# The first batch without split operands and in a new written order, and the last tile's ending in halves

## The chip, the cores and the metric

The kernel runs on one core of one Trainium2 chip. The metric is device microseconds of one execution, the median over runs. A core has TensorE (PE, matmuls from SBUF into PSUM), VectorE (DVE), ScalarE (ACT), GpSimd (POOL) and SyncE (SP, which issues most DMAs here). Each engine works through its own queue in order, and waits on semaphores for what others produce.

## The reference

```python
def _attn_ref(q, k, v, p):                  # 8 batches, 8 heads, 576 tokens, 64 wide; p: 32 packing queries
    def sm_attn(qq, kk, vv):
        s = scale * np.matmul(qq, kk.transpose(0, 1, 3, 2))
        s = s - np.max(s, axis=-1, keepdims=True)
        a = np.exp(s)
        a = a / (np.sum(a, axis=-1, keepdims=True) + 1e-09)
        return np.matmul(a, vv)
    p_packed = sm_attn(p, k, v)             # 32 x 64 per head
    return sm_attn(q, p_packed, p_packed)

def _moe_ref(x, w_ch1, w_ch2):              # x: 8 x 576 x 512, the heads side by side
    X = np.fft.fft(np.fft.fft(x, axis=1), axis=2)
    u = x + np.real(X).astype(np.float32)
    mu = np.mean(u, axis=-1, keepdims=True)
    var = np.mean((u - mu) ** 2, axis=-1, keepdims=True)
    un = (u - mu) / np.sqrt(var + 1e-06)
    ch = np.maximum(un @ w_ch1, 0.0) @ w_ch2     # 512 -> 2048 -> 512
    return u + ch
```

## The kernel before

**Tiles.** Every two batches give nine blocks of 128 rows of `u`; four blocks make a tile of 512 rows, so the eight batches make nine tiles. For each tile `ffn` runs 16 steps: `up` (L910, 12 matmuls into the PSUM bank `ph`), Relu into a high part `hh` (ACT) and a low part `hl` (DVE, L917), and `down` of the step before (L927, 12 matmuls into `acc0` to `acc3`). All of this is fp32r (one pass) with each operand split into a rounded high part and the rest: three matmuls stand for one. The helper `split` (L107 copies the high part on ACT, L110 subtracts on DVE or POOL) makes the parts; `wsplits` makes those of the weights (`wr_h`, `wr_l`). After the last step the block is scaled and added (L975, DVE) and stored (L976, SP's queue).

**The front.** `front(b)` makes the blocks of batch b: scores of the packing queries (`s`), their exponentials (`e`), turned by PE (`e1tp`, `e1tq`, copied into `e1T`), packed values (`po`, `pp`), transposed (`pptp`, copied into `ppT`), scores of the 576 queries (`s2T`, turned by DVE into `s`), maximum `m`, exponentials, sum `z`, mean `d`, weights turned back (`a`). Everything comes for two groups g of four heads. Even and odd folds (`eo`, `f`) of the weights take the place of the first transform; `pg` times `turn` gives the spectrum of the packed values (`turned`, joined pairwise into `gh`, `gl`). Products `py` of folds and value spectra, summed over both groups (`first_products`, L702 to L708), give `yh`, `yl` and a remainder `yr`; these times the tables `tbh`, `tbl`, `tbr` give the spectra `pz` (L280 to L282, L632), copied to SBUF (`spec`). The plain values `px` (folds times the spread packed values `bdh`, `bdl`) and the spectra make `pe`, `qe`, and from these the four row blocks in `ubuf` with their row sums (L774 to L783). ACT subtracts the mean (`un`, L994), PE turns the block (`untp`), ACT and DVE split it (`uh`, `ul`), and the first `up` starts.

**What sets the order.** For batches 1 to 7 the front is spread over the steps of the tile ahead. For batch 0 nothing runs yet, and the strings of `ORDER` write the order of PE, DVE, ACT and POOL out by hand: a letter is a part (`parts`), the number its group or argument. Letters used below: `s x t p b d` scores, exponentials, turned scores, packed values, their spread, their transpose; `q e m a` second scores, less maximum, less mean, weights; `g j` value spectrum and its join; `f r` folds and the folds' rest; `h H F J n l` low and high parts; `P X` first products and first values; `w v` two ways to unpack a weight chunk (ACT, DVE), `W K V Q` loads; `i` idle matmuls (`i203`: 20 of them, gated by entry 3 of `gates`), which compute nothing that is used. `T0` to `T2` load tables by POOL's DMA queue. The order of SP's queue is not written by hand. The work on weight chunks is spread over batch 0's front and the first tile (`TOPS`, `BITS`, `fetch`).

PSUM has eight banks: `bank` hands out `acc0` to `acc3` and three others in turn during the first batch; `ph` is single.

Of the kernel before, what the change touches and what calls it, by code (L numbers as in the profile page):

```python
# [83 lines left out]
def tile_kernel(ctx, tc, kpT, qT, v, w1, w2, tabH, tabL, tabR, tabF, tabB, tabT, sel, ident_d, out):  # L84
# [199 lines left out]
    def front(b):  # L284
# [130 lines left out]
        def packed(g):  # L415
# [30 lines left out]

            in_place("b", g, spread)

        def packed_parts(g):
# [7 lines left out]
            hi = work.tile([P, P], F32R, tag="pph", name="pph")  # L457
            lo = work.tile([P, P], F32R, tag="ppl", name="ppl")
            nc.scalar.copy(hi, tp[:, :P])
            in_place("l", g, lambda: nc.vector.tensor_tensor(lo, tp[:, :P], hi.bitcast(F32), ALU.subtract))  # L460
            pph[g], ppl[g] = hi, lo
# [32 lines left out]
        def less_mean(g):  # L494

            z = small.tile([P, 18], F32, tag="z18", name="z18")
            d = small.tile([P, 18], F32, tag="d18", name="d18")
            nc.vector.tensor_reduce(z, s2s[g], AX.X, ALU.add)
            nc.vector.tensor_scalar(d, z, 1.0 / NPK, None, ALU.mult)
            nc.vector.tensor_scalar(z, z, float(NPK), 1e-9, ALU.add, ALU.add)  # L500
# [4 lines left out]
        def values_spectrum(g):

            hi = work.tile([P, 2, N2], F32R, tag="gh", name="gh")
            lo = work.tile([P, 2, N2], F32R, tag="gl", name="gl")
# [16 lines left out]
            def join():  # L525
                for t in range(2):
                    TW[TA[min(b, 2)]].tensor_tensor(prod[0][:, t, :], prod[0][:, t, :], prod[1][:, t, :], ops[t])
                if b == 0:
                    nc.scalar.copy(hi, prod[0])
                    late["J", g] = lambda: nc.vector.tensor_tensor(lo, prod[0], hi.bitcast(F32), ALU.subtract)  # L530
                else:
# [15 lines left out]
        def folded(g):  # L547
# [10 lines left out]
            eos[g], fs[g] = eo, f  # L558

        def folded_rest(g):  # L560
# [29 lines left out]
            nc.scalar.activation(xh[g], ec[:, 0:256], AF.Copy, bias=1.0 / 16)  # L590
            oh[g] = work.tile([P, 256], F32R, tag="oh", name="oh")
            nc.scalar.copy(oh[g], oc[:, 0:256])

        def folded_high(g):
            fh[g] = work.tile([P, FW], F32R, tag="fh", name="fh")
            nc.scalar.copy(fh[g], fs[g])

        def folded_parts(g):
# [9 lines left out]

            def low():
                fl[g] = work.tile([P, FW], F32R, tag="fl", name="fl")  # L610
                nc.vector.tensor_tensor(fl[g], f, fh[g].bitcast(F32), ALU.subtract)
# [15 lines left out]
        def spectrum(t, q, tag=None):  # L627
# [3 lines left out]
            three(pz[:, :N2], tbh[t][:, w], tbl[t][:, w], yh[t][:, q, :], yl[t][:, q, :], True, False)  # L631
# [534 lines left out]
```

## Time and profile before

| | |
|---|---|
| median of 3 runs | 965.59 us (965.23 to 966.66) |
| the profiled execution | 964.36 us |
| its span | 962.2 us |
| PE busy | 944.4 us, 98% of the span |
| DVE, ACT, POOL busy | 589.5, 452.3, 463.2 us |
| mean granted PE clock | 0.998 |

The span is the time from the first to the last record; the execution's own time lies some 2 us above it. Rows of a timeline give the start, the length (of a merged row: from the first start to the last end), engine, line, operation, what it writes and reads, and in brackets the idle time of the engine ahead of it and who ended it. A matmul's length includes its way through the array; matmuls in a row start closer together than they are long. A plain f32 matmul appears as two rows (passes).

### The profile page before, as it was taken

What the parts mean: (1) busy time and instruction counts of PE and PEld (TensorE: products, weight loads), DVE (VectorE), ACT (ScalarE), POOL (GpSimd) and SP (SyncE); (2) the same over time, 40 slices, a digit from 0 to 9 for tenths busy, and PEclk for the clock granted to TensorE, in tenths of its full rate; (3) what the DMA queues carried; (4) which work ended last, traced back from release to release, by engine and by line L of the source; (5) the groups of instructions that cost most, each with busy time, mean ns of one, the idle gap of its engine ahead of it and who ended that gap; (6) DMA issues with size and microseconds to landing.
All of it is one profiled execution on the core that took longest, in us unless ns stands there. A gap on an engine that the chain in (4) does not pass through costs nothing.

```text
span 962.2 us, 15191 instructions
## 1 busy us (share of the span) xinstructions
PE 944.4 (98%) x5614; PEld 774.4 (80%) x5614; DVE 589.5 (61%) x1186; ACT 452.3 (47%) x930; POOL 463.2 (48%) x397
## 2 busy tenths in 40 slices
PE   7899999999999999999999999999999999999997
PEld 4777887788778887788778877888778888887886
DVE  5989967684667756794668466874679353123112
ACT  5689564444434444444444444454444443233331
POOL 3156534653555435643465355543555355445442
PEclk9999999999999999999999999999999999999999
DMA  9675125400340016200540045100600011001001
GB/s 358 220 268 190 42 84 164 136 1 1 128 152 37 1 44 209 85 1 25 165 148 0 1 140 166 55 1 23 212 30 23 16 50 44 22 23 45 1 0 44
DMA packets 48777, 80.74 MB, mean 84 GB/s; under 512 B 7088, under 2 KB 28464, under 8 KB 48704
## 3 DMA queue, kind: packets, MB, share of 16 engines
q1 hardware_dynamic: 42480, 69.62, 21.3%
q10 hardware_dynamic: 5184, 8.85, 2.9%
q0 software_dynamic: 1040, 1.31, 0.5%
q8 instruction: 44, 0.72, 0.3%
q14 instruction: 29, 0.24, 0.1%
HBM read 59.45 MB, written 20.32 MB: 83 GB/s over the span
## 4 chain that ended last, share of the span: by engine, by line
PE 93%; DVE 3%; ACT 2%; DMA 1%; issue 1%; ACTq 0%; DVEq 0%
PE acc L927 40%; PE ph L910 40%; PE po L424 1%; PE px L282 1%; PE px L280 1%; PE px L281 1%; PE s2T L329 1%; PE py L282 1%; PE py L280 1%; PE py L281 1%; PE s L329 1%; ACT e L356 1%; PE idle L730 1%; PE pz L653 0%; DMA kp<-kpT 0%
## 5 line engine op out<-in xcount | busy, mean ns | idle before, releaser
L110 POOL TENSOR_TENSOR wr_l<-w2f,wr_h 128x512 fp32r<-128x512 f32 x144 | 188.2, 1307 | 275.8 <-ACT wr_h L107 269.8
L110 POOL TENSOR_TENSOR wr_l<-w1f,wr_h 128x512 fp32r<-128x512 f32 x144 | 200.3, 1392 | 195.2 <-ACT wr_h L107 175.6
L917 DVE SCALAR_TENSOR_TENSOR hl<-ph,hh 128x512 fp32r<-128x512 f32 x144 | 98.7, 686 | 288.3 <-ACT hh L916 287.6
L910 PE MATMUL ph<-uh,wr_h 128*128 128x512 f32 (+1 forms) x580 | 226.1, 392 | 1.0 <-ACT uh L107 1.0
L927 PE MATMUL acc<-wr_h,hh 128*128 128x512 f32 x576 | 226.0, 392 | 0.0
L927 PE MATMUL acc<-wr_h,hl 128*128 128x512 f32 x576 | 224.8, 390 | 0.0
L927 PE MATMUL acc<-wr_l,hh 128*128 128x512 f32 x576 | 224.8, 390 | 0.0
L910 PE MATMUL ph<-ul,wr_h 128*128 128x512 f32 (+1 forms) x580 | 224.2, 388 | 0.5 <-DVE ul L110 0.5
L910 PE MATMUL ph<-uh,wr_l 128*128 128x512 f32 (+1 forms) x580 | 224.1, 388 | 0.0
L916 ACT ACTIVATE hh<-ph 128x512 fp32r<-128x512 f32 x144 | 86.2, 598 | 235.6 <-PE ph L910 221.7
L107 ACT CAST wr_h<-w1f 128x512 fp32r<-128x512 f32 x144 | 89.3, 620 | 185.2 <-POOL wr_l L110 79.3
L910 PEld LDWEIGHTS ph<-uh,wr_h 128*128 128x128 f32 x580 | 108.5, 188 | 29.3 <-DVE s L479 5.9
L927 PEld LDWEIGHTS acc<-wr_h,hl 128*128 128x128 f32 x576 | 108.1, 188 | 23.2
L910 PEld LDWEIGHTS ph<-uh,wr_l 128*128 128x128 f32 x580 | 108.5, 188 | 22.7
L910 PEld LDWEIGHTS ph<-ul,wr_h 128*128 128x128 f32 x580 | 108.6, 188 | 21.6 <-DVE ul L110 0.9
L927 PEld LDWEIGHTS acc<-wr_h,hh 128*128 128x128 f32 x576 | 108.2, 188 | 21.7
L927 PEld LDWEIGHTS acc<-wr_l,hh 128*128 128x128 f32 x576 | 108.2, 188 | 20.9
L107 ACT CAST wr_h<-w2f 128x512 fp32r<-128x512 f32 x144 | 88.3, 613 | 34.1 <-PE acc L927 26.8
L975 DVE SCALAR_TENSOR_TENSOR ubuf<-acc,stat,ubuf 128x512 f32<-128x512 f32 x36 | 24.6, 744 | 3.5 <-PE acc L927 3.5
L834 DVE TENSOR_SCALAR unp<-ubuf,stat 128x512 f32<-128x512 f32 x28 | 25.4, 907 | 1.0 <-POOL bdl L110 0.7
L254 ACT ACTIVATE junk<-ubuf,stat 128x512 f32<-128x512 f32 x36 | 25.8, 717 | 0.2 <-DVE stat L249 0.2
L110 DVE TENSOR_TENSOR yl<-py,yh 128x258 fp32r<-128x258 f32 x32 | 13.2, 425 | 18.5 <-ACT yh L107 17.8
(230 smaller groups left out, 1216.7 us busy)
## 6 DMA issues: line engine op xcount, KB each, us to landing
kp<-kpT SPq DMA_DIRECT2D x16, 608.0 KB, 4.3
out<-ubuf SPq DMA_DIRECT2D x36, 256.0 KB, 3.9
far<-unt SPq DMA_DIRECT2D x28, 256.0 KB, 2.0
back<-far SPq DMA_DIRECT2D x112, 64.0 KB, 2.0
qt<-qT ACTq DMA_DIRECT2D x12, 576.0 KB, 4.6
vt<-v SPq DMA_DIRECT2D x12, 512.0 KB, 3.8
w1f<-w SPq DMA_DIRECT2D x9, 512.0 KB, 6.6
w2f<-w SPq DMA_DIRECT2D x9, 512.0 KB, 6.4
```

Of the source, the lines that this page charges most:

```text
L107: copied = nc.scalar.copy(hi, src)
L110: (lo_eng or nc.vector).tensor_tensor(lo, src, hi.bitcast(F32), ALU.subtract)
L254: nc.scalar.activation(junk, u, AF.Square, bias=st[:, 1:2], scale=-sign, accum_out=st[:, 2:3])
L280: nc.tensor.matmul(o, lh, rh, start=first, stop=False)
L281: nc.tensor.matmul(o, lh, rl, start=False, stop=False)
L282: nc.tensor.matmul(o, ll, rh, start=False, stop=last)
L834: nc.vector.tensor_scalar(un, u_of[key].rearrange("p (c q d) -> p q c d", c=4, q=4), stat_of[key][:, 1:2], None, ALU.subtract)
L910: nc.tensor.matmul(ph[:, t], l[:, c * P:(c + 1) * P], r[:, c, t], start=(k == 0), stop=(k == 11))
L916: nc.scalar.activation(hh[:, :T], ph[:, :T], AF.Relu)
L917: nc.vector.scalar_tensor_tensor(hl[:, :T], ph[:, :T], 0.0, hh[:, :T].bitcast(F32), ALU.max, ALU.subtract)
L927: nc.tensor.matmul(acc[i], l[:, w], r, start=(j == 0 and k == 0), stop=(j == NJ - 1 and k == 2))
L975: nc.vector.scalar_tensor_tensor(u, acc[i], stat_of[keys[i]][:, 2:3], u, ALU.mult, ALU.add)
```

## The change

**In batch 0** the split parts go: `f`, `eo` copies (`xh`, `oh`), `gh`, `bd`, `ppT` and `y` stay plain f32, and each product is one plain f32 matmul in the place of two or three fp32r ones. The table for the spectra is loaded whole (`tabS`, into a place of the weight buffer that a query tile had); the split tables, which batch 1 needs first, load later. `gh` is written by the join. [...] Statistics of a row block follow it at once.

**In all batches** `less_mean` subtracts the mean by one fused instruction where DVE does it.

**In the last tile** the last two `down` are interleaved, the last accumulator is made in halves of 256 columns, and the scaling goes in the order of the accumulators, the last in halves, stored from two queues (SP and ACT).

**The written order** of batch 0 changes (first lines of the diff): `d0 q0` stand ahead of `t1`; the joins `j` ahead of the folds' rest `r`; the second group's folds come ahead of its sum's rest; three idle blocks go.

```diff
-ORDER = ("K0 K1 V0 I0 Q0 W0 V1 Q1 B0 W1 W2 W3 i70 s0 x0 s1 i40 t0 x1 w0 p0 b0 T0 t1 n0 d0 v0 z0 i20 W4 W5 W6 W7 W8 W9 q0 e0 p1 "
-         "b1 T1 T2 i80 l0 d1 w1 w2 w3 w4 m0 q1 a0 e1 g0 i122 l1 f0 r0 w5 F0 m1 n1 g1 w6 w7 i203 a1 j0 w8 h0 J0 H0 P0 f1 r1 F1 i64 j1 h1 J1 X0 "
-         "H1 v2 W10 P1",
+ORDER = ("K0 K1 V0 I0 Q0 W0 V1 Q1 B0 W1 W2 W3 i70 s0 x0 s1 i40 t0 u0 x1 w0 p0 b0 T0 d0 u1 v0 q0 t1 z0 W4 W5 W6 W7 W8 W9 e0 p1 b1 "
+         "T1 i80 d1 w1 w2 w3 m0 q1 a0 e1 w4 g0 i122 f0 c0 j0 r0 w5 m1 g1 P0 w6 w7 a1 f1 c1 j1 X0 r1 w8 c2 "
+         "v2 W10 P1 T2",
...
+            whole.append(spot(0, 7, [P, 2, KT]))
+            todo = [(whole[0], tabS.rearrange("t p n -> p t n"))] + [(tbr[t], tabR[t]) for t in range(2)] + [(tbf, tabF)]
...
-                nc.vector.tensor_copy(t[:, 4, :], tq[:, g * P:(g + 1) * P])
+                (nc.scalar.copy if b == 0 and g else nc.vector.tensor_copy)(t[:, 4, :], tq[:, g * P:(g + 1) * P])
...
+            def plain_spread():
+                bdh[g] = work.tile([P, 4 * D], F32, tag="bdh", name="bd")
+                nc.gpsimd.tensor_tensor(bdh[g].rearrange("p (a d) -> p a d", a=4), pp2[:, 0:1, :].to_broadcast([P, 4, D]),
+                                        bmask.unsqueeze(2).to_broadcast([P, 4, D]), ALU.mult)
...
-            nc.vector.tensor_scalar(d, z, 1.0 / NPK, None, ALU.mult)
-            nc.vector.tensor_scalar(z, z, float(NPK), 1e-9, ALU.add, ALU.add)
-            nc.vector.reciprocal(z, z)
-            engs[g].tensor_tensor(s2s[g], s2s[g], broadcast(d), ALU.subtract)
-            zs[g] = z
+            if engs[g] is nc.gpsimd:
+                d = small.tile([P, 18], F32, tag="d18", name="d18")
+                nc.vector.tensor_scalar(d, z, 1.0 / NPK, None, ALU.mult)
+                nc.gpsimd.tensor_tensor(s2s[g], s2s[g], broadcast(d), ALU.subtract)
+                nc.vector.tensor_scalar(total, z, float(NPK), 1e-9, ALU.add, ALU.add)
+            else:
+                (nc.vector if b else nc.gpsimd).tensor_scalar(total, z, float(NPK), 1e-9, ALU.add, ALU.add)
+                nc.vector.scalar_tensor_tensor(s2s[g], broadcast(z), -1.0 / NPK, s2s[g], ALU.mult, ALU.add)
+            nc.vector.reciprocal(total, total)
+            zs[g] = total
...
-                three(px[:, g * 256:(g + 1) * 256], ah[g][:, w], al[g][:, w], bdh[g], bdl[g], True, True)
+                if b:
+                    three(px[:, g * 256:(g + 1) * 256], ah[g][:, w], al[g][:, w], bdh[g], bdl[g], True, True)
+                else:
+                    nc.tensor.matmul(px[:, g * 256:(g + 1) * 256], ah[g][:, w], bdh[g], start=True, stop=True)
...
-            outs = [(0, 0), (0, 2), (1, 0), (1, 2), (0, 1), (1, 1)]
+            outs = [(0, 0), (1, 0), (0, 2), (1, 2), (0, 1), (1, 1)]
...
-                nc.tensor.matmul(py[:nr, :N2], fh[g][:, w], gh[g][:, t, :], start=(g == 0), stop=False)
-                nc.tensor.matmul(py[:nr, :N2], fh[g][:, w], gl[g][:, t, :], start=False, stop=False)
-                if g == 0:
-                    nc.tensor.matmul(py[:nr, :N2], fl[g][:, w], gh[g][:, t, :], start=False, stop=False)
...
+                nc.tensor.matmul(py[:nr, :N2], fh[g][:, w], gh[g][:, t, :], start=(g == 0), stop=(g == 1))
...
+        def early_values():
+            for n in "pq":
+                held = work.tile([P, 2, N2], F32, tag="gl", name="px")
+                nc.scalar.copy(held[:, :, 0:256], halves(ypx[n, 0]))
+                ypx[n, 0] = held[:, :, 0:256]
...
+            if nxt is None and j == NJ - 1:
+                pairs = [ready.pop(0), None]
+                down(j - 1, *prev, pair=pairs[0], to=(0, 1, 2))
+                pairs[1] = ready.pop(0)
+                for k, i in ((1, 0), (0, 3), (1, 1), (1, 2), (1, 3)):
+                    down(j - 1 + k, *(prev, cur)[k], pair=pairs[k], to=(i,))
+                break
...
-        for i in (2, 3, 0, 1):
+        for i in (2, 3, 0, 1) if nxt is not None else range(4):
             u = u_of[keys[i]]
-            nc.vector.scalar_tensor_tensor(u, acc[i], stat_of[keys[i]][:, 2:3], u, ALU.mult, ALU.add)
-            nc.sync.dma_start(out[(first + i) * P:(first + i + 1) * P, :], u)
+            for cols in (slice(0, DM // 2), slice(DM // 2, DM)) if nxt is None and i == 3 else (slice(0, DM),):
+                nc.vector.scalar_tensor_tensor(u[:, cols], acc[i][:, cols], stat_of[keys[i]][:, 2:3], u[:, cols],
+                                               ALU.mult, ALU.add)
+                (nc.sync if cols.start == 0 else nc.scalar).dma_start(out[(first + i) * P:(first + i + 1) * P, cols], u[:, cols])
```

DVE's queue before, from the second group's product with its weights: `a` is its transpose, `turned` the join of group 0, `eo` the second group's folds.

```order
L539 TENSOR_TENSOR s_341<-s_341,z_399 128x576
L541 STREAM_TRANSPOSE a<-s_341 128x576
L527 TENSOR_TENSOR turned<-turned 128x258 x2
L605 SCALAR_TENSOR_TENSOR xl<-eo,xh 128x256
L607 TENSOR_TENSOR ol<-eo,oh 128x256
L530 TENSOR_TENSOR gl<-turned,gh 128x516
L611 TENSOR_TENSOR fl<-f,fh 128x776
L554 TENSOR_TENSOR eo<-a 128x287
L555 TENSOR_TENSOR eo<-a 128x287
```

The same place now:

```order
L552 TENSOR_TENSOR s_322<-s_322,t_379 128x576
L554 STREAM_TRANSPOSE a<-s_322 128x576
L567 TENSOR_TENSOR eo<-a 128x287
L568 TENSOR_TENSOR eo<-a 128x287
L569 TENSOR_TENSOR f<-eo 128x2x128
L570 TENSOR_TENSOR f<-eo 128x2x128
L543 TENSOR_TENSOR gh<-turned 128x258 x2
L587 TENSOR_TENSOR f<-eo 128x2x3x15 x2
```

The folds follow the transpose at once, the low parts are gone, the join of group 0 has gone further ahead, and that of group 1 stands ahead of its folds' rest (L587).

PE's queue before, from the idle block that waits for the second group's maximum to the first products:

```order
L730 MATMUL idle<-ubuf,m_347 18x128 x12
L514 MATMUL pg<-basis,pph 128x258
L516 MATMUL pg<-basis,ppl 128x258
L514 MATMUL pg<-basis,pph 128x258
L516 MATMUL pg<-basis,ppl 128x258
L730 MATMUL idle<-ubuf,z_399 18x128 x20
L702 MATMUL py<-gh,fh 128x258
L703 MATMUL py<-gl,fh 128x258
L705 MATMUL py<-gh,fl 128x258
```

The same place now, to the second group's first products:

```order
L751 MATMUL idle<-ubuf,m_328 18x128 x12
L532 MATMUL pg<-basis,ppT 128x258 x2
L723 MATMUL py<-gh,f 128x258 x2
L723 MATMUL py<-gh,f 101x258
L723 MATMUL py<-gh,f 99x258
L723 MATMUL py<-gh,f 128x258 x2
L697 MATMUL px<-bd,xh 128x256 x2
L697 MATMUL px<-bd,oh 128x256 x2
L723 MATMUL py<-gh,f 128x258 x2
```

The block of 20 idle matmuls is gone, and 6 plain matmuls stand for 18.

DVE's queue at the very end, before (`acc_9446` to `acc_9449` are the four accumulators in their order):

```order
L975 SCALAR_TENSOR_TENSOR ubuf<-acc_9448,stat,ubuf 128x512
L975 SCALAR_TENSOR_TENSOR ubuf<-acc_9449,stat,ubuf 128x512
L975 SCALAR_TENSOR_TENSOR ubuf<-acc_9446,stat,ubuf 128x512
L975 SCALAR_TENSOR_TENSOR ubuf<-acc_9447,stat,ubuf 128x512
L1162 UNCONDITIONAL_BRANCH
```

And now (`acc_9301` to `acc_9304`):

```order
L1010 SCALAR_TENSOR_TENSOR ubuf<-acc_9301,stat,ubuf 128x512
L1010 SCALAR_TENSOR_TENSOR ubuf<-acc_9302,stat,ubuf 128x512
L1010 SCALAR_TENSOR_TENSOR ubuf<-acc_9303,stat,ubuf 128x512
L1010 SCALAR_TENSOR_TENSOR ubuf<-acc_9304,stat,ubuf 128x256 x2
L1198 UNCONDITIONAL_BRANCH
```

The third accumulator stood first, now the first does, and the fourth comes in two halves.

More of the change, by code (lines that the diff above doesn't have):

```diff
@@ L83, in tile_kernel @@
 @with_exitstack
-def tile_kernel(ctx, tc, kpT, qT, v, w1, w2, tabH, tabL, tabR, tabF, tabB, tabT, sel, ident_d, out):
+def tile_kernel(ctx, tc, kpT, qT, v, w1, w2, tabS, tabH, tabL, tabR, tabF, tabB, tabT, sel, ident_d, out):
     nc = tc.nc
@@ L456, in packed_parts @@
             ppT[g] = t
[L457 to L461, printed above, removed]
+            if b:
+                hi = work.tile([P, P], F32R, tag="pph", name="pph")
+                lo = work.tile([P, P], F32R, tag="ppl", name="ppl")
+                split(hi, lo, tp[:, :P])
+                pph[g], ppl[g] = hi, lo
         def broadcast(x):
@@ L601, in folded_parts @@
             ec, oc = eo[:, 0, :], eo[:, 1, :]
-            if g not in fh:
-                folded_high(g)
+            fh[g] = work.tile([P, FW], F32R, tag="fh", name="fh")
+            nc.scalar.copy(fh[g], f)
             xl[g] = work.tile([P, 256], F32R, tag="xl", name="xl")
@@ L630, in spectrum @@
             w = slice(P * q, P * q + P)
[L631 removed]
+            if b:
+                three(pz[:, :N2], tbh[t][:, w], tbl[t][:, w], yh[t][:, q, :], yl[t][:, q, :], True, False)
+            else:
+                nc.tensor.matmul(pz[:, :N2], whole[0][:, t, w], yh[t][:, q, :], start=True, stop=False)
             nc.tensor.matmul(pz[:, :N2], tbr[t][:NRC[t], w], yr[t][:NRC[t]], start=False, stop=True)
+            if b == 0 and q == 0:
+                return pz
             sb = (ffp if tag else work).tile([P, N2], F32, tag=tag or f"spec{t}", name=f"spec{t}", bufs=6 if tag else 1)
@@ L661, in spectra_apart @@
                 remainders(True, False)
-                strips([[yh[t].bitcast(F32), yl[t].bitcast(F32)] for t in range(2)], False, True)
+                strips([[yh[t]] for t in range(2)], False, True)
             sbs = []
@@ L764, in front @@
             yr.append(st)
-            whole = work.tile([P, 2, N2], F32, tag=("ysum", "gh")[t], name="ysum", bufs=1 + t)
+            total = work.tile([P, 2, N2], F32, tag=("ysum", "gh")[t], name="ysum", bufs=1 + t)
             for c in range(2):
-                nc.scalar.copy(whole[:, c, :], pys[c][:, :N2])
-            ysum.append(whole)
+                nc.scalar.copy(total[:, c, :], pys[c][:, :N2])
+            ysum.append(total)
             yield
@@ L918, in up, with down @@
             return hh, hl
-        def down(j, hh, hl, moves=()):
+        def down(j, hh, hl, moves=(), pair=None, to=range(n)):
             moves = list(moves)
-            vh, vl = ready.pop(0)
-            for i in range(n):
+            vh, vl = pair or ready.pop(0)
+            for i in to:
                 w = slice(i * P, (i + 1) * P)
-                for k, (l, r) in enumerate(((hh, vh), (hh, vl), (hl, vh))):
-                    nc.tensor.matmul(acc[i], l[:, w], r, start=(j == 0 and k == 0), stop=(j == NJ - 1 and k == 2))
-                    if moves:
-                        moves.pop(0)()
+                halved = nxt is None and j == NJ - 1 and i == n - 1
+                for cols in (slice(0, DM // 2), slice(DM // 2, DM)) if halved else (slice(0, DM),):
+                    for k, (l, r) in enumerate(((hh, vh), (hh, vl), (hl, vh))):
+                        nc.tensor.matmul(acc[i][:, cols], l[:, w], r[:, cols], start=(j == 0 and k == 0),
+                                         stop=(j == NJ - 1 and k == 2 and cols.stop == DM))
+                        if moves:
+                            moves.pop(0)()
         def less(*ks):
@@ L1126, in _prepare @@
     }
-    for n, t in zip(("tabH", "tabL", "tabR", "tabF", "tabB", "tabT", "sel", "ident_d"), _tables()):
+    for n, t in zip(("tabS", "tabH", "tabL", "tabR", "tabF", "tabB", "tabT", "sel", "ident_d"), _tables()):
         arrays[n] = t
```

104 lines of the change are left out of this document (53 added, 51 removed).

## The prediction

> **What bounds the kernel now.** I read the page's chain first, then busy time by stage, then each engine's order of time at the two ends.
>
> ```profile
> PE 93%; DVE 3%; ACT 2%; DMA 1%; issue 1%; ACTq 0%; DVEq 0%
> ```
>
> ```profile
> 0.00:48.59 48.59, 38.83 (x366) 29.95 (x366) 36.84 (x97) 29.33 (x61) 12.97 (x32) 0.96 0.77 286
> 48.59:956.73 908.14, 905.56 (x5248) 744.43 (x5248) 550.53 (x1087) 422.94 (x869) 450.22 (x365) 1.00 0.22 72
> 956.73:962.20 5.47, 0.00 (x0) 0.00 (x0) 2.18 (x4) 0.00 (x0) 0.00 (x0) 0.92 0.51 192
> ```
>
> Columns: stretch, length, busy time (instructions) of PE, weight loads, DVE, ACT, POOL, then the granted clock, DMA share, GB/s. Between the first feed-forward matmul (48.59) and the end of the last (956.73) PE is busy for 905.56 of 908.14 us: this stretch shrinks only if its matmuls do. Ahead of it lie 48.59 us of one batch's attention and spectra, part of PE's work there being idle matmuls; behind it 5.47 us without any. The gain must come from these two ends.
>
> DVE carries the second half of the first end (start, length, line, what):
>
> ```profile
> 16.67 0.29 DVE L455 COPY ppT<-pptp 128x128 f32<-128x128 f32 x1 [0.22 <-PE pptp L453]
> 17.51 0.75 DVE L498 TENSOR_REDUCE z<-s 128x18 f32<-128x576 f32 x1 [0.55 <-ACT s L490]
> 18.30 0.24 DVE L499 TENSOR_SCALAR d<-z 128x18 f32<-128x18 f32 x1
> 18.58 0.18 DVE L500 TENSOR_SCALAR z<-z 128x18 f32<-128x18 f32 x1
> ...
> 20.34 0.72 DVE L539 TENSOR_TENSOR s<-s,z 128x576 f32<-128x576 f32 x1
> ...
> 21.79 0.71 DVE L485 TENSOR_REDUCE m<-s 128x18 f32<-128x576 f32 x1
> ...
> 28.70 1.25 DVE L539 TENSOR_TENSOR s<-s,z 128x576 f32<-128x576 f32 x1
> 29.98 0.78 DVE L541 STREAM_TRANSPOSE a<-s 128x576 f32<-128x576 f32 x1
> 30.68 0.72 DVE L527 TENSOR_TENSOR turned<-turned 128x258 f32<-128x258 f32 x2
> 31.32 0.42 DVE L605 SCALAR_TENSOR_TENSOR xl<-eo,xh 128x256 fp32r<-128x256 f32 x1
> ...
> 32.10 0.70 DVE L530 TENSOR_TENSOR gl<-turned,gh 128x516 fp32r<-128x516 f32 x1
> 32.71 0.96 DVE L611 TENSOR_TENSOR fl<-f,fh 128x776 fp32r<-128x776 f32 x1
> ...
> 33.95 0.45 DVE L555 TENSOR_TENSOR eo<-a 128x287 f32<-128x287 f32 x1
> ...
> 43.08 0.68 DVE L774 TENSOR_TENSOR pe<-px,spec 128x512 f32<-128x512 f32 x1
> 43.68 0.41 DVE L779 TENSOR_TENSOR qe<-px,spec 128x256 f32<-128x256 f32 x1
> ```
>
> What to see: between the second group's transpose (29.98) and its fold (eo) stand group 0's join and low halves, and `pe`, the first step to the output rows, starts at 43.08. What follows `pe` ends in two PE rows, the first half and the second half of the first feed-forward step:
>
> ```profile
> 34.07 0.42 ACT L590 ACTIVATE xh<-eo 128x256 fp32r<-128x256 f32 x1 [0.88 <-DVE eo L554]
> ...
> 45.87 1.33 ACT L994 ACTIVATE un<-ubuf,stat 128x512 f32<-128x512 f32 x2 [1.61 <-DVE stat L249]
> ```
>
> ```profile
> 48.59 0.74 PE L910 MATMUL ph<-uh,wr_h 128*128 128x256 f32 x4 [0.68 <-ACT uh L107]
> ...
> 51.61 0.74 PE L910 MATMUL ph<-uh,wr_h 128*128 128x256 f32 x4 [0.34 <-ACT uh L107]
> ```
>
> **The price of a plain f32 matmul.** Batch 0 gives up the split into a rounded high part and a low part: where three fp32r matmuls (two, for `pg`) stood, one plain f32 matmul stands. Rows:
>
> ```profile
> 14.25 2.05 PE L730 MATMUL idle<-ubuf 128*128 128x128 f32 x16
> ...
> 22.55 4.46 PE L730 MATMUL idle<-ubuf,m 128*18 128x128 f32 x24 [2.48 <-DVE m L485]
> ...
> 27.62 4.54 PE L730 MATMUL idle<-ubuf,z 128*18 128x128 f32 x40
> ```
>
> ```profile
> 34.11 0.12 PE py L702
> 34.23 0.12 PE py L703
> 34.36 0.12 PE py L705
> ```
>
> An idle matmul is plain f32, and the trace counts two passes for each: 40 passes of 128 columns in 4.54 us are 0.1135 each, so 0.227 for 128 columns and 0.457 for 258. Three fp32r matmuls of 258 columns are 0.36. So PE gets dearer, by 0.10 per group of three; the gain is on DVE and ACT, which no longer make the low and high parts. No 128-row f32 matmul of 258 columns is in the trace; the four-strip f32 rows below give 1.01 / 2 = 0.50 per such set, so 0.46 to 0.50; I take 0.457, the same 128x128 shape.
>
> **The front, station by station** (times of the profiled run; "now" is my estimate).
>
> 1. First group's scores ahead: its packed transpose stands right after `po`, no longer behind the second group's turned scores; that saves about 0.7 on the way to its maximum. But DVE's queue has the second `ppT` copy ahead of `z`, and PE does 16 idle passes (2.05 in the row above) before the transpose that it needs. The second `po` comes some 0.75 later, so `ppT` starts at about 17.2 (16.67 before), `z` at 17.4 (17.51). Only 0.1 is left.
> 2. The rewritten `less_mean`: `d` and the addition for `z` leave DVE's queue, and the subtraction becomes one fused instruction of the same 128x576 shape. 0.24 + 0.18 less; with step 1, `m` ends at 22.0 instead of 22.5. The added POOL instruction (128x18) is hidden beside the fused one, if POOL is through with its table loads, now four instead of seven.
> 3. The PE block gated by `m` still takes 4.46 (24 passes at 0.186), so `pg` and the second group's products move by the same 0.5 only; the join of group 0 (0.72), now earlier in the queue, fills what was a wait. The transpose `a`: 29.2 (29.98). The L539 row of 1.25 ran beside a POOL split that is gone; at 0.72, like the same row of group 0, it would add 0.5. I take 0.3 of it.
> 4. `eo` straight behind `a`: the join, two low halves of 0.34, `gl` and `fl` (33.59 - 30.68 = 2.9 in all by the starts) are gone from between. The odd fold ends at 30.7 (34.40): 3.7 ahead.
> 5. From there PE is the chain. ACT's `xh` and `oh` copies (0.42 each) let the four `px` matmuls start at 31.1; 4 x 0.454 = 1.82 ends them at 32.95; six `py` of group 1, 6 x 0.457 = 2.74, end at 35.7. The join and the folds' rest (DVE, to 33.0) lie beside `px`. ACT's copies of `px` and `y` lie beside `py`, except the last. Then the first spectrum, 0.457 + 0.12, and 0.16 until it can be read: `pe` reads it in PSUM at 36.5. Before it was 43.08: 6.6 ahead.
> 6. The statistics of each row block now follow at once; the first `un` starts earlier, the second starts at `pe` + 3.1 and ends at + 3.8, where before it ended at + 4.1 (45.87 + 1.33 - 43.08). First `ph`: 41.7 (48.59). In the second pair the two statistics stand between the row blocks on DVE and cost 0.1 to 0.2 each; second half of `ph` at 45.0 (51.61). I take **6.6** for the front.
>
> Costed at nothing: the later-needed tables (`tabH`, `tabL`), put in POOL's queue behind group 1's mean, where the trace shows POOL without work (its next row waited 21.33 us); the whole table `tabS` (256 KB) in a place where a query tile was, needed at 35.7, some 15 us after its issue; batch 1's query loads, which SP now issues behind weight chunk W10, itself waiting for DVE's `v2` (33.7): they are read only in the first feed-forward tile.
>
> ```profile
> 50.67 1.29 POOL L110 TENSOR_TENSOR wr_l<-w1f,wr_h 128x512 fp32r<-128x512 f32 x1 [21.33 <-ACT wr_h L107]
> ```
>
> **In the first tile.** The remainder's strips of `yl` fall away and `px` of the remainder is 2 x 0.454 instead of 6 x 0.12:
>
> ```profile
> 53.55 1.01 PE pz L653 x16
> ```
>
> Half of 1.01 gone, 0.19 added: **0.3**.
>
> **The tail.**
>
> ```profile
> 956.34 0.39 PE L927 MATMUL acc<-wr_h,hl 128*128 128x512 f32 x1
> ```
>
> ```profile
> 956.16 2.75 DVE L975 SCALAR_TENSOR_TENSOR ubuf<-acc,stat,ubuf 128x512 f32<-128x512 f32 x4 [3.52 <-PE acc L927]
> ```
>
> ```profile
> DMA to landing us min/median/max: 2.0/2.1/2.1
> ```
>
> All four output blocks are scaled after the third accumulator is done: DVE ends at 958.91, 2.18 behind PE's 956.73. Now accumulator 0 is complete 15 matmul slots before the end, 1 six, 2 three, and the last is done in halves. DVE then has only the second half left at PE's end: 0.1 wait + 0.41 (the 256-column row `qe`, which also reads PSUM), with the first half just ahead, so DVE ends some 0.75 behind PE, at most 0.04 of which is the six half matmuls. 2.18 - 0.75 = **1.4**, between 1.0 (a backlog of half a block) and 1.7. The two half stores leave on two queues; I give their landing nothing, since a store takes 2.0 to 2.1 in that row whatever its place.
>
> Sum: 6.6 + 0.3 + 1.4 = 8.3. The profiled run took 964.36 (span 962.2), 1.23 below the median 965.59, so 956.1 for its like, and 957.3 beside the median.
>
> [...] The new order drops 28 of 59 idle matmuls, 26 of them in the two blocks around the first products (20, the 40 passes above, and 6). Clock by microseconds:
>
> ```profile
> 21.00:22.00 1.00, 0.00 (x0) 0.00 (x0) 0.97 (x3) 0.93 (x3) 0.00 (x0) 1.00 1.14 400
> 22.00:23.00 1.00, 0.45 (x3) 0.34 (x4) 1.00 (x2) 0.56 (x2) 0.35 (x1) 0.82 1.14 397
> 23.00:24.00 1.00, 1.00 (x7) 0.69 (x6) 1.00 (x4) 1.00 (x3) 0.80 (x1) 0.50 1.12 387
> ```
>
> A wait of 2.48 us was enough for a clock of 0.50, which lasted until 26. Now PE waits about 1.8 there, and 0.9 ahead of `px`. [...]
>
> **Rivals.**
> - The clock falls ahead of the PE-bound stretch (31 to 40). At half speed for 3.4 us, as from 22.6 to 26.0, it loses 1.7: 959.0; twice, 960.7. For it: the 2.48 row, and the idles that are gone. Against: PE is busy for some 3.5 us right before the 0.9. 0.12.
> - More than summed: the L539 stretch goes wholly, the clock does not fall at 22 (PE has less to wait), the tail gives 1.7: 8.3 + 0.2 + 1.2 + 0.3 = 10.0, 955.6. 0.12.
> - DVE's queue in the first tile takes it back. The bank `ph` is single, so each step waits for the last `hl`:
>
> ```profile
> 86.19 1.79 DVE L203 SCALAR_TENSOR_TENSOR w1f<-w1f 128x512 int32<-128x512 int32 x1
> 87.90 0.68 DVE L917 SCALAR_TENSOR_TENSOR hl<-ph,hh 128x512 fp32r<-128x512 f32 x1
> ```
>
> ```profile
> 89.10 2.72 PE ph L910 x12
> ```
>
> `hl` ends at 88.58, 0.52 before PE needs the bank. One more row stretched beside POOL (1.79 against 0.68) costs 0.6 in a step; in six steps 3.6: 960.9. Against: all of it is ordered relative to the first `ph` and moves with it; only the 0.3 of PE above is lost to the margin. 0.07.
> - Slower: the clock stays at half through the start of the feed-forward. To pass 965.59 by 0.2% it has to lose 8.3 + 1.9 = 10.2, that is 20.4 us of PE at half; at 21 us it would be 967.8. The one fall of the trace lasted 3.4. 0.03.
> - That the front does not get shorter, because a tile is waited for whole (`py` for the folds' rest, `pe` for both spectra): `py` would start at 33.1 instead of 32.95, `pe` at 37.1: 0.6, inside the range.
>
> **How the numbers follow.** The forecast holds 0.66 (its own range 956.0 to 958.6), the clock 0.12, more 0.12, DVE's queue 0.07, slower 0.03. The range 954.9 to 960.3 takes in the larger gain, one fall of the clock and part of the next. 0.2%, 1.9 us, is about what a measurement tells from no change; all cases but the last lie beyond it, with a little left for mishaps added up: faster 0.95, same 0.02, slower 0.03.
>
> **What would show it.** `pe` near 36.5 and both `ph` near 41.7 and 45.0; plain f32 `py` at 0.23 per pass; the second group's `eo` directly behind `a`; no clock below 1.00 after 27; from the first `ph` to PE's end about 907.8 (908.14 less 0.3); DVE's last row 0.75 behind PE's. The prediction is wrong if PE or DVE waits between 27 and 36 for something that I have as ready (a bank, `tabS`, a weight chunk on ACT), if f32 passes of 258 columns are slower than by the idle rows, or if PE shows waits between 60 and 120.

## The result, and the profile after

| | before | after | forecast |
|---|---|---|---|
| median of 5 runs each, us | 966.21 (965.23 to 966.66) | 956.64 (955.98 to 957.91) | 957.3 (954.9 to 960.3) |
| the profiled execution, us | 964.36 | 956.59 | 956.1 |
| its span, us | 962.2 | 954.5 | |

The ratio is 0.9907 [0.9893, 0.9921]: faster, by 7.6 to 10.3 us. The profiled executions differ by 7.8 and their spans by 7.7. The profiled execution of before lay 1.85 below the median of its five runs, that of after at its median, so the working below goes by the spans and accounts for 7.7; the medians lie 9.6 apart.

The stretches of after, cut at the same events as those of before (stretch, length, busy time and instructions of PE, weight loads, DVE, ACT, POOL, granted clock, DMA share, GB/s):

```profile
0.00:42.29 42.29, 33.94 (x287) 24.28 (x287) 29.07 (x79) 26.57 (x54) 12.99 (x32) 0.96 0.90 334
42.29:950.12 907.83, 906.17 (x5241) 744.85 (x5241) 551.95 (x1077) 423.10 (x869) 448.32 (x365) 1.00 0.22 73
950.12:954.50 4.38, 0.00 (x0) 0.00 (x0) 0.98 (x3) 0.00 (x0) 0.00 (x0) 1.00 0.50 180
```

The first stretch is 42.29 where it was 48.59 (6.30 less), the middle 907.83 where it was 908.14 (0.31 less), the last 4.38 where it was 5.47 (1.09 less): 7.70 in all. The forecast's first `ph` at 41.7 stands for 6.9 in the first stretch; by the second half of that step it had 6.6, then 0.3 in the first tile, and 1.4 at the end.

PE after, from the first value spectra to the two halves of the first feed-forward step, and the last matmul (start, length, engine, line, what, and the wait ahead):

```profile
20.71 1.11 PE L532 MATMUL pg<-basis,ppT 128*128 128x258 f32 x4 [1.94 <-DMA basis<-tabB]
...
23.08 4.33 PE L751 MATMUL idle<-ubuf,m 128*18 128x128 f32 x24 [1.26 <-DVE m L494]
...
28.32 2.78 PE L723 MATMUL py<-gh,f 128*128 128x258 f32 x12
...
31.85 0.71 PE L697 MATMUL px<-bd,xh 128*128 128x256 f32 x2 [0.32 <-ACT xh L612]
...
34.04 2.44 PE L723 MATMUL py<-gh,f 128*128 128x258 f32 x10 [0.18 <-DVE f L600]
36.33 0.60 PE L648 MATMUL pz<-y,w1f 128*128 128x258 f32 x2
...
42.29 0.74 PE L933 MATMUL ph<-uh,wr_h 128*128 128x256 f32 x4 [0.67 <-ACT uh L107]
...
45.49 0.74 PE L933 MATMUL ph<-uh,wr_h 128*128 128x256 f32 x4 [0.35 <-ACT uh L107]
...
949.84 0.28 PE L952 MATMUL acc<-wr_h,hl 128*128 128x256 f32 x1
```

The block of 20 idle matmuls between the second `pg` and `py` is gone, and the first products of group 0 run where it stood. From the odd fold to the spectra PE waits 0.32 and 0.18 only.

DVE after, the rows that answer to those of before, and its last rows:

```profile
17.25 0.29 DVE L464 COPY ppT<-pptp 128x128 f32<-128x128 f32 x1 [1.54 <-PE pptp L462]
17.46 0.74 DVE L507 TENSOR_REDUCE z<-s 128x18 f32<-128x576 f32 x1
18.24 0.76 DVE L515 SCALAR_TENSOR_TENSOR s<-z,s 128x576 f32<-128x576 f32 x1
19.98 0.27 DVE L516 RECIPROCAL t<-t 128x18 f32<-128x18 f32 x1 [0.98 <-POOL t L514]
...
22.32 0.71 DVE L494 TENSOR_REDUCE m<-s 128x18 f32<-128x576 f32 x1
...
30.08 0.78 DVE L554 STREAM_TRANSPOSE a<-s 128x576 f32<-128x576 f32 x1
30.89 0.46 DVE L567 TENSOR_TENSOR eo<-a 128x287 f32<-128x287 f32 x1
31.27 0.45 DVE L568 TENSOR_TENSOR eo<-a 128x287 f32<-128x287 f32 x1
...
37.08 0.69 DVE L795 TENSOR_TENSOR pe<-px,pz 128x512 f32<-128x512 f32 x1 [0.54 <-PE pz L649]
...
947.49 0.75 DVE L1010 SCALAR_TENSOR_TENSOR ubuf<-acc,stat,ubuf 128x512 f32<-128x512 f32 x1 [1.48 <-PE acc L952]
948.85 2.25 DVE L1010 SCALAR_TENSOR_TENSOR ubuf<-acc,stat,ubuf 128x512 f32<-128x512 f32 x4 [0.61 <-PE acc L952]
```

`pe` starts at 37.08 (43.08 before). The row to notice is the reciprocal: DVE stood still for 0.98 us for an addition of 128x18 that had been given to POOL. After it no DVE row up to 34 shows a wait, so DVE's queue carries those 0.98 on to `m`, `a` and `eo`. POOL's own rows say why the addition was late:

```profile
15.08 1.52 POOL L110 TENSOR_TENSOR wr_l<-w1f,wr_h 128x512 fp32r<-128x512 f32 x1 [2.53 <-ACT wr_h L107]
16.56 0.61 POOL L441 TENSOR_TENSOR bd<-pp,bmask 128x256 f32<-128x256 f32 x1
17.12 0.80 POOL L145 DMA_DIRECT2D w1f<-tabS  x1
17.91 1.10 POOL L145 DMA_DIRECT2D tbr<-tabR  x2
18.98 0.57 POOL L145 DMA_DIRECT2D tbf<-tabF  x1
19.63 0.31 POOL L514 TENSOR_SCALAR t<-z 128x18 f32<-128x18 f32 x1
```

`z` was there at 18.20 (17.46 + 0.74). POOL was issuing four loads from 17.12 until 19.55, and only then could it add. The weight split ahead of them began at 15.08, where it began at 13.72 before, because ACT's second copy into `e1T`, which stands ahead of the high part, came at 13.72 instead of 11.83. But most of these 1.36 us fell into a wait that POOL had before as well, and the loads began only 0.24 later than before (17.12, 16.88). Before, two of POOL's rows:

```profile
16.33 0.61 POOL L434 TENSOR_TENSOR bd<-pp,bmask 128x256 f32<-128x256 f32 x1 [1.31 <-DVE pp L429]
...
18.51 0.56 POOL L139 DMA_DIRECT2D tbh<-tabH  x1
```

The second is the fourth of the seven loads there. It ends at 19.07, also behind `z`.

### The profile page after: what moved, and what is told of

Same layout as the page of the kernel before. It is cut to its first block, busy times and chain, and to the rows that moved or that the text cites. A ratio compares the mean times of both kernels' runs of the same rounds, so it can differ in the third digit from the quotient of the medians.

```text
span 954.5 us, 14981 instructions
## 1 busy us (share of the span) xinstructions
PE 940.1 (98%) x5527; PEld 769.1 (81%) x5527; DVE 582.0 (61%) x1156; ACT 449.7 (47%) x923; POOL 461.3 (48%) x397
## 4 chain that ended last, share of the span: by engine, by line
PE 93%; DVE 2%; ACT 1%; DMA 1%; issue 1%; POOL 0%; ACTq 0%; DVEq 0%
PE acc L952 40%; PE ph L933 40%; PE po L431 1%; PE px L288 1%; PE px L286 1%; PE px L287 1%; PE s2T L335 1%; PE py L286 1%; PE py L287 1%; PE py L288 1%; PE s L335 1%; DMA e1T<-fare 1%; ACT e L362 1%; PE idle L751 0%; DMA kp<-kpT 0%
## 5 line engine op out<-in xcount | busy, mean ns | idle before, releaser
L110 POOL TENSOR_TENSOR wr_l<-w1f,wr_h 128x512 fp32r<-128x512 f32 x144 | 198.1, 1376 | 188.0 <-ACT wr_h L107 169.2
L933 PEld LDWEIGHTS ph<-uh,wr_h 128*128 128x128 f32 x580 | 108.5, 188 | 29.2 <-DVE s L488 5.9
L1010 DVE SCALAR_TENSOR_TENSOR ubuf<-acc,stat,ubuf 128x512 f32<-128x512 f32 (+1 forms) x37 | 24.8, 730 | 2.1 <-PE acc L952 2.1
L264 POOL TENSOR_TENSOR stat<-stat,mhalf 128x1 f32<-128x1 f32 x36 | 24.7, 698 | 0.0
L552 DVE TENSOR_TENSOR s<-s,t 128x576 f32<-128x576 f32 x16 | 24.0, 1499 | 0.4
```

Source lines behind the costliest of these rows:

```text
L110: (lo_eng or nc.vector).tensor_tensor(lo, src, hi.bitcast(F32), ALU.subtract)
L264: nc.gpsimd.tensor_tensor(st[:, 2:3], st[:, 2:3], mhalf, ALU.pow)
L552: engw[g].tensor_tensor(s2s[g], s2s[g], broadcast(zs[g]), ALU.mult)
L933: nc.tensor.matmul(ph[:, t], l[:, c * P:(c + 1) * P], r[:, c, t], start=(k == 0), stop=(k == 11))
L1010: nc.vector.scalar_tensor_tensor(u[:, cols], acc[i][:, cols], stat_of[keys[i]][:, 2:3], u[:, cols], ALU.mult, ALU.add)
```

## The experiments

The before kernel ran beside each. Two readings are used throughout: the start of the first `ph`, and `pe` less the start of group 0's `z`, which takes out that a run begins a little earlier or later. Of before they are 48.59 and 25.57, of after 42.29 and 19.62. Each reading comes from one profiled execution.

**1. The tail alone.** The before kernel with only the edits of the last tile (`down` with `pair`, `to` and halves, the interleaved last two steps, the scaling in halves with stores on two queues), as in the diff above.

> The kernel before with only the last tile's edits (interleaved last steps, last accumulator in halves, scaling in the order of the accumulators, two store queues). Theory: from the last matmul's end to the span's end 4.4 us instead of 5.5, as in the changed kernel, and nothing else moves: span 1.1 us shorter, ratio about 0.999. Rival: the tail's gain comes from the shorter run as a whole (an earlier DMA state, say), and the edit alone gives less than 0.3 us.

Ratio 0.9989 [0.9979, 0.9998], 964.2 against 965.8: faster by 0.2 to 2.0 us. From PE's end to the span's end 4.08 (5.47 before), and DVE ends 0.97 behind PE, as in after. The tail is worth about 1.1 to 1.4; the other 6 to 7 us come from the front. This run also shows what blurs such comparisons: its profiled span (963.7) is longer than that of before although the tail is shorter, because the clock fell twice in it, at 21.1 for twice as long as in before, and once more at the first `ph`, which ran at half speed:

```profile
48.90 1.22 PE L910 MATMUL ph<-uh,wr_h 128*128 128x256 f32 x4 [0.68 <-ACT uh L107]
...
53.00 0.74 PE L910 MATMUL ph<-uh,wr_h 128*128 128x256 f32 x4 [0.20 <-ACT uh L107]
```

**2. Plain operands in the old written order.** After, with the idle blocks of 20, 6 and 2 and the old places of the parts:

```diff
-ORDER = ("... t0 u0 x1 w0 p0 b0 T0 d0 u1 v0 q0 t1 z0 W4 ... W9 e0 p1 b1 "
-         "T1 i80 d1 w1 w2 w3 m0 q1 a0 e1 w4 g0 i122 f0 c0 j0 r0 w5 m1 g1 P0 w6 w7 a1 f1 c1 j1 X0 r1 w8 c2 "
+ORDER = ("... t0 u0 x1 w0 p0 b0 T0 t1 u1 d0 v0 z0 i20 W4 ... W9 q0 e0 p1 b1 "
+         "T1 i80 d1 w1 w2 w3 w4 m0 q1 a0 e1 g0 i122 f0 r0 c0 w5 m1 g1 w6 w7 i203 a1 j0 w8 P0 f1 r1 c1 i64 j1 X0 c2 "
```

> The changed kernel's plain operands, spectra in PSUM and tail, with batch 0's parts written in the order of before (low parts left out, both idle blocks of 20 and 6 kept). Theory: the plain f32 products are dearer on PE and stand behind the idle blocks, so PE sets the pace: pe near 41, first ph near 46.5, span near 958.8; more than half of the front's gain is missing. Rival: dropping the low parts is the gain and the order adds little: first ph at 43.5 or less.

Ratio 0.9971 [0.9960, 0.9983]; first `ph` 47.27, span 959.3 (the theory had 46.5 and 958.8). Plain operands, spectra read in PSUM and the fused `less_mean` alone move the first `ph` by 1.32. Taking the low parts off DVE and ACT frees time there, but PE still works through its block of idle matmuls first, and `py` waits for it:

```profile
28.42 4.54 PE L751 MATMUL idle<-ubuf,t 128*18 128x128 f32 x40
32.89 2.88 PE L723 MATMUL py<-gh,f 128*128 128x258 f32 x12
35.61 1.50 PE L751 MATMUL idle<-ubuf,eo 128*128 128x128 f32 x12
```

**3. The same without `i203` and `i64`.**

```diff
-... w6 w7 i203 a1 j0 w8 P0 f1 r1 c1 i64 j1 X0 c2 "
+... w6 w7 a1 j0 w8 P0 f1 r1 c1 j1 X0 c2 "
```

> As the one with the old order, but without the idle blocks of 20 and 6. Theory: of what the new order brings, most is the dropped idle blocks (4 us of the first ph), and the moves of joins, scores and folds are worth about 1: pe near 38, first ph near 43.3, span near 955.5. Rival one: without the idle blocks PE's clock falls in the old order too and takes it back: clock 0.5 between 28 and 40, first ph at 45 or later. Rival two: the moves themselves carry the gain: first ph at 45 or later at full clock.

Ratio 0.9938 [0.9917, 0.9958]; first `ph` 44.37, 1.1 later than the theory had it, and not where the rivals had it. Now PE stands idle where the block was, because the join of group 0 comes behind the second group's transpose in DVE's queue:

```profile
31.35 2.88 PE L723 MATMUL py<-gh,f 128*128 128x258 f32 x12 [2.74 <-DVE gh L543]
```

So the front is a ladder: 48.59, plain operands 47.27 (1.32), idle blocks out 44.37 (2.90), new written order 42.29 (2.08); the theory of run 3 had 4 and about 1 for the last two. Each was measured on top of the one before: with the join further ahead in DVE's queue, `py` starts at 28.32 instead of 31.35. The moves within the new order were not run one by one, and the new order with the idle blocks kept was not run. The clock was at half for 6.8 us in runs 2 and 3 and for 3.4 in before and after, and the steps of the ladder carry that too. By the ratios of the medians the same three steps are worth 2.8 (the tail with it), 3.2 and 3.0 us, and that of run 3 is uncertain by 2.0.

**4. The sum on VectorE.** After, with the addition for `z` back on DVE:

```diff
-                (nc.vector if b else nc.gpsimd).tensor_scalar(total, z, float(NPK), 1e-9, ALU.add, ALU.add)
+                nc.vector.tensor_scalar(total, z, float(NPK), 1e-9, ALU.add, ALU.add)
```

> The changed kernel, but the 18-column addition for the first group's reciprocal is on DVE again, not on POOL behind four table loads. Theory: DVE's wait of 0.98 us ahead of the reciprocal was the part of the front that the forecast missed: the second group's maximum ends 0.7 to 0.8 earlier (22.2 instead of 23.0), pe starts near 36.4 instead of 37.1, the first ph near 41.6 instead of 42.3, span 953.8. Rival: the wait is covered, because the basis table lands only at 20.7 and the idle block and ACT's weight chunks hold the chain anyway: ph stays within 0.2 of 42.3.

Ratio 0.9902 [0.9887, 0.9917]; `pe` less `z` is 18.48 (19.62 in after), first `ph` 41.19, earlier than the theory's 41.6. The span is 953.9, only 0.6 less than after's although PE ends 1.49 earlier: the last store took 3.1 to land here and 2.0 in after. DVE and PE of this run:

```profile
19.03 0.26 DVE L516 RECIPROCAL t<-t 128x18 f32<-128x18 f32 x1
...
21.37 0.71 DVE L494 TENSOR_REDUCE m<-s 128x18 f32<-128x576 f32 x1
```

```profile
20.00 1.11 PE L532 MATMUL pg<-basis,ppT 128*128 128x258 f32 x4 [1.18 <-DMA basis<-tabB]
22.13 2.80 PE L751 MATMUL idle<-ubuf,m 128*18 128x128 f32 x24 [1.03 <-DVE m L494]
```

The wait at the reciprocal is gone. But the clock did not fall here either (the 24 idle passes took 2.80, not 4.33), so this run alone doesn't say which of the two brought the 1.14.

**5. The clock held, the sum left on GpSimd.** After with two more idle blocks, one behind the second group's scores and one behind the first `pg` (a single run):

```diff
-... m0 q1 a0 e1 w4 g0 i122 f0 ...
+... m0 q1 i100 a0 e1 w4 g0 i60 i122 f0 ...
```

> The changed kernel with 10 more idle matmuls after the second group's scores and 6 after the first group's value spectrum, so that PE's clock does not fall at 23 us; the addition for the reciprocal stays on POOL. It tells the two readings of the run with that addition on DVE apart, in which the clock also stayed at 1.00. Theory (the addition's wait was the cost): clock 1.00 from 20 to 40, the idle block takes 2.8 instead of 4.3 us, but DVE's chain is as before: z of the second group at 26.7, pe at 36.8 to 37.1. Rival (the clock was the cost): pe at 36.2 or earlier.

955.92 us. The clock stayed at 1.00, DVE still waited for POOL, and `pe` less `z` is 19.43. `pe` itself, at 36.59, lies between the two figures expected; the run's `z` began 0.30 earlier than after's (17.16), and with that added it is 36.89, the theory's:

```profile
19.65 0.27 DVE L516 RECIPROCAL t<-t 128x18 f32<-128x18 f32 x1 [0.95 <-POOL t L514]
```

```profile
23.05 2.80 PE L751 MATMUL idle<-ubuf,m 128*18 128x128 f32 x24
```

With the runs below this closes a table of `pe` less `z`:

| | clock fell at about 22 | clock held |
|---|---|---|
| addition on GpSimd | 19.62 (after) | 19.43 (this) |
| addition on VectorE | 18.70, 18.69 (runs 7, 9) | 18.48, 18.47 (runs 4, 8) |

The addition costs 0.92 to 0.96 in either column, the clock 0.19 to 0.23 in either row. The 4.33 us block does not matter much, since DVE's queue carries that stretch.

**6. No idle block at all ahead of the second `pg`.** After without `i122` (a single run):

```diff
-... w4 g0 i122 f0 c0 ...
+... w4 g0 f0 c0 ...
```

> The changed kernel without the 12 idle matmuls that wait for the second group's maximum, so that PE has nothing to do from about 22 to 26.7 us. Rival of the prediction (the clock): PE's clock is 0.5 when the first products start and stays there through the second group's products: pe at 38.5 or later (37.1 in the changed kernel). Theory: the clock is 0.5 for about 3.4 us of the first group's products only, which end near 31.4, and the second group's px wait for xh at 31.9 in any case: pe between 36.8 and 37.6.

958.1 us. The clock was at half for twice as long, and PE waited for the join:

```profile
27.65 5.37 PE L723 MATMUL py<-gh,f 128*128 128x258 f32 x12 [4.54 <-DVE gh L543]
32.87 1.02 PE L697 MATMUL px<-bd,xh 128*128 128x256 f32 x4
```

Read literally, `pe` at 38.30 is the rival's figure more nearly than the theory's. But this run began late: its clock had been at half from about 11.9 to 15.3 as well (its mean clock is 0.994, that of after 0.998), and its `z` started at 19.06, 1.6 behind after, before any part of the edit. `pe` less `z` is 19.24, 0.38 less than in after, of which 0.21 is a shorter wait for POOL's addition (0.77). So a fall that long cost nothing at `pe` here; `px` already ran at the full clock. One run with a late start is no proof that the block can go.

**7. A last tile without a backlog on DVE.** Run 4 with the accumulators finished earlier:

```diff
-                for k, i in ((1, 0), (0, 3), (1, 1), (1, 2), (1, 3)):
+                for k, i in ((1, 0), (1, 1), (1, 2), (0, 3), (1, 3)):
```

> The addition on DVE, and in the last tile the third accumulator's last step ahead of the fourth's last but one. Theory: DVE has the third block scaled 0.5 us earlier, so it ends 0.55 us behind PE instead of 0.98; with the front's 1.1 us, span 952.9 to 953.4, ratio near 0.989. Rival: the last two half blocks are bound by their own matmuls and the queue, DVE still ends 0.9 behind PE.

Ratio 0.9904 [0.9889, 0.9918], 955.86 us, no gain over run 4: the rival's number came out. DVE is through with three accumulators well ahead of PE's end (949.03), yet it ends as late behind it as before:

```profile
946.39 2.10 DVE L1010 SCALAR_TENSOR_TENSOR ubuf<-acc,stat,ubuf 128x512 f32<-128x512 f32 x3 [1.48 <-PE acc L952]
949.13 0.88 DVE L1010 SCALAR_TENSOR_TENSOR ubuf<-acc,stat,ubuf 128x256 f32<-128x256 f32 x2 [0.64 <-PE acc L952]
```

```profile
948.39 0.28 PE L952 MATMUL acc<-wr_h,hl 128*128 128x256 f32 x1
...
948.75 0.28 PE L952 MATMUL acc<-wr_h,hl 128*128 128x256 f32 x1
```

The first half's last matmul ended at 948.67 (948.39 + 0.28), but its scaling started at 949.13, 0.10 behind the end of the second half's. So the first half waited for more than its own matmuls, which the rival had named. Both scalings come behind PE: 950.01 less 949.03 is 0.98. In after DVE was in a backlog instead: its last four scalings ran from 948.85 to 951.10 without a wait, and that also ended 0.98 behind PE. By these rows either is enough for the 0.98.

**8. The same with the clock held.** Run 7 with the two idle blocks of run 5.

> As the one before, with the 16 more idle matmuls. Theory: the scatter of the runs (3 us in the kernel before) comes from falls of PE's clock in the first 55 us; with PE filled until the products start, every run has a mean clock of 0.998 or more and the runs lie within 1 us, median near 955. Rival one: the fill delays the first group's value spectrum and the maximum's block, pe 0.5 us later than without it. Rival two: the scatter has another cause and stays 2 us or more.

Ratio 0.9906 [0.9889, 0.9923], 956.26 us; first `ph` 41.28. Four runs, with mean clocks of 0.999 to 1.0, still lie between 955.65 and 957.33, 1.68 apart where the theory had 1 and rival two 2 or more. Rival one did not show: `pe` less `z` is 18.47, not longer than run 7's 18.70. So something other than falls of the clock spreads the runs of this kernel; what it is stays open.

**9. The halves in two banks.** Run 7 with the fourth accumulator's second half in the bank of `ph` in the last tile (a single run):

```diff
+        other = psf.tile([P, 512], F32, tag="ph", name="acc3b") if nxt is None else None
+        def part(i, cols):
+            return other[:, :DM // 2] if nxt is None and i == n - 1 and cols.start else acc[i][:, cols]
...
-            pool, tag = (ps, "ps") if alone and j % 2 else (psf, "ph")
+            pool, tag = (ps, "ps") if nxt is None or alone and j % 2 else (psf, "ph")
...
-                halved = nxt is None and j == NJ - 1 and i == n - 1
+                halved = nxt is None and i == n - 1
```

> The version with the sum on VectorE and the reordered last tile, and in the last tile the two 256-column halves of the fourth accumulator stand in two PSUM banks for all 16 steps (the first-layer products of that tile take turns in the three shared banks instead). Theory (the first half can't be read while PE still writes the second half of the same bank, so both scalings of 0.4 to 0.5 lie behind PE's last matmul): with two banks the first half is scaled beside PE's last three matmuls, and VectorE ends 0.50 to 0.62 behind PE's end instead of 0.98; the row of the last two scalings shows the first starting ahead of PE's end. Rival (the first half is late for another reason, such as the latency from a matmul's end to VectorE's start): VectorE still ends 0.9 to 1.0 behind. The halved fourth accumulator costs PE 15 x (6 x 0.117 - 3 x 0.228) = 0.3 us, so the span is expected to be equal within 0.4; the front (first ph about 41.0 to 42.3) is untouched.

958.15 us, span 956.1. DVE's last two rows, and PE's:

```profile
951.18 0.48 DVE L1014 SCALAR_TENSOR_TENSOR ubuf<-acc,stat,ubuf 128x256 f32<-128x256 f32 x1 [0.32 <-PE acc L956]
951.58 0.47 DVE L1014 SCALAR_TENSOR_TENSOR ubuf<-acc3b,stat,ubuf 128x256 f32<-128x256 f32 x1
```

```profile
950.78 0.28 PE L956 MATMUL acc<-wr_h,hl 128*128 128x256 f32 x1
...
951.15 0.28 PE L956 MATMUL acc3b<-wr_h,hl 128*128 128x256 f32 x1
```

The first scaling starts 0.12 behind its own last matmul (951.06) and 0.25 ahead of PE's end (951.43); DVE ends 0.62 behind PE. The theory held for the tail: the halves that shared a bank were waited for together (in run 7 the first scaling starts 0.10 behind the end of the second half's matmuls), those in two banks were not (here it starts 0.25 ahead of it). The two halves here are also two tiles and two accumulation groups, and the run does not separate these from the bank. The 0.36 by which DVE ends nearer to PE (0.98 less 0.62) was not a gain of the whole, and the span was not equal within 0.4 as expected: it is 2.0 longer than run 7's, and PE ends 2.40 later. PE waited 1.8 ahead of `po` where run 7 shows 0.8, a step of the last tile took 5.50 instead of 5.44 (0.9 in all, where 0.3 was expected), and the first `ph` came 0.18 later.

## Why the prediction was right, and where it was off

**The place and the size.** 7.7 by the spans where the sum had 8.3: the gain lies at the two ends, and the middle moved with the first `ph` (907.83; the forecast was about 907.8). The median came out 0.66 below the forecast although the sum was 0.6 too large. The forecast took it that the profiled execution of after would lie below its median as that of before did, by 1.23; it lay at its median (956.59 and 956.64). That error is larger than the sum's and of the other sign, so part of the nearness is luck.

**Step 1** held: `z` at 17.46 (17.4).

**Step 2 failed.** "Hidden beside the fused one, if POOL is through with its table loads": the condition was named and not worked out. POOL got through at 19.63, DVE waited 0.98, and `m` ended at 23.03 (22.0 forecast, 22.51 before). Run 4 with the addition on DVE has it end at 22.08, which is the forecast. Counting loads, four instead of seven, was not enough. The fused instruction was expected to end at about 18.9 (17.4 + 0.75 + 0.76), and in the trace of before the fourth load ends at 19.07; with 0.31 for the addition, a wait of some 0.5 was there to be read, by this estimate. The other half came from loads that began 0.24 later and took 0.24 longer (2.43 us from the first start to the last end, 2.19 for the first four before).

**Steps 3 and 4** held in their order and lengths, shifted by step 2's miss: `a` at 30.08 (29.2), the odd fold's end at 31.72 (30.7), with `eo` directly behind `a`. The block gated by `m` took 4.33 (4.46), but step 3 had it set the pace of `a`, and run 5 shows that it hardly does: 1.5 us less of it brought 0.19. DVE's queue had no wait there. The row of 1.25 fell to 0.75, the whole 0.5 of which step 3 took 0.3.

**Step 5** gave back part of it. From the odd fold's end to `pe` the forecast was 5.8; it took 5.36. Plain passes of 258 columns are cheaper than taken: twelve in 2.78 and two in 0.60 make (2.78 - 0.60) / 10 = 0.218 a pass, so 0.437 a matmul and not 0.457. And one of the four `px` matmuls ran at 30.94, ahead of the wait for `xh`. `pe` at 37.08 (36.5).

**Step 6** held: from `pe` to the first `ph` 5.21 (5.2), to the second half 8.41 (8.5). The statistics between the row blocks took 0.15 each. Front: 6.1 at the second half, 6.3 at the first (6.6 and 6.9 forecast).

**The first tile**: 904.63 from the second half of `ph` to the last matmul's end, 905.12 before: 0.5 where 0.3 was taken.

**The tail**: 1.09 where 1.4 was taken. "DVE then has only the second half left at PE's end" is the step that failed: it had both halves left, and ended 0.98 behind PE, not 0.75. The prediction counted 15 matmul slots from the end of accumulator 0 to PE's end; in full matmuls, as its six and three are counted, they are 12, so there was less room for DVE's scalings of 0.75. The lower end given for it, 1.0 by a backlog of half a block, was near, and a backlog was there. It was not the only hindrance: run 7 took the backlog away and nothing changed, run 9 took the shared bank away as well and 0.36 went. Landings of 2.0 were as priced in after; from DVE's end to the span's end it took 3.40 (3.29 before), another 0.11.

**The rivals.** The clock did fall, but in the idle block ahead of the PE-bound stretch, as before; from 27 on it stayed at 1.00. It fell to 0.50 at 22.9, with waits of 1.94 and 1.26 us there, neither as long as the one of 2.48 us in before. DVE's queue in the first tile took nothing back: between 60 and 120 PE shows no wait. A front that does not get shorter was ruled out by `pe`, and nothing decided for the slower one. The part of "more than summed" that was there to be had is run 4's 1.1 in the trace.

**What is not shown.** Runs 4 and 7 (955.99 and 955.86) and after (956.64) overlap in their runs; that moving the addition makes the whole faster is seen in the trace of the front only. What the fused `less_mean` and the single moves of the new order bring by themselves was not run.

## What to carry to other kernels

When a small instruction is moved to another engine to relieve a queue, work out when that engine is through with what stands ahead of it, its DMA issues included: here a row of 0.18 us on VectorE became 0.31 on GpSimd and came 1 us late, and the relieved engine waited longer than the work took. Look at idle blocks that are there to keep a clock up together with the order (16 more idle matmuls held it at 1.00 in run 5, where it fell to 0.50 in after): here a block of 4.5 us stood where the products could go; without it they began 1.5 us earlier, and 3.0 earlier still with the join moved ahead as well. Halves of a result that were to overlap its last step were waited for together in one PSUM bank (run 7, DVE 0.98 behind PE), and apart in two banks and two tiles (run 9, 0.62).
